# Lending a matmul accumulator bank between two sums in a fused attention and mixture-of-experts kernel

## The chip, the cores and the metric

The kernel runs on one core of one Trainium2 chip. The metric is the device time of one execution in microseconds (us). TensorE (PE) multiplies and writes only into PSUM, which here is used as eight banks of 128 x 512 fp32. VectorE (DVE) and ScalarE (ACT) read results out of PSUM; GpSimd (POOL) works on SBUF; SyncE (SP) issues DMAs. Each engine takes its instructions in the order in which the program lists them. Engines wait for one another by semaphores.

## The reference

Agent attention over 4 batches of 11456 tokens of width 128, with 49 agents per batch, and then a mixture of 8 experts of which each token takes one:

```python
a2k = softmax(scale * agents @ k.T);  agent_v = a2k @ v        # 49 x 128 per batch
q2a = softmax(scale * q @ agents.T);  x = q2a @ agent_v        # 11456 x 128 per batch
logits = x @ w_gate;  e = argmax(logits);  g = softmax(logits)[e]
out = g * (relu(x @ w1[e]) @ w2[e])                            # w1: 128 x 1024, w2: 1024 x 128
```

All inputs and outputs are fp32.

## The kernel before

Each batch is cut into 12 chunks: eleven of 1024 tokens and a last one of 192. For one chosen expert per batch the product of agent values and `w1` is formed once (`Ah` and `Al`, the high and low fp16 halves), so that layer 1 of a token is a product with its 49 attention weights. Those weights stand in `M`. Tokens that chose another expert are done in blocks at the end.

**The main stream.** The function `experts(b)` goes over 23 groups of four 128-token tiles (the last of a batch holds two 96-token tiles), and within a group over 8 slices `f` of the 1024 hidden units. One pair of group and slice is a *step*: 184 steps a batch, 736 in all. A step is `layer1` (two 512-column matmuls into a bank `ph`, L1535 and L1536; then ACT writes the high half of `hh`, L1538, and DVE the low half, L1539, which frees the bank) and, five steps later (`LAG = 5`), `layer2` (12 matmuls of 128 columns into the bank `py`, L1553). Eight steps make one *sum* in `py`. When a sum is complete DVE drains it with one multiplication, `yo<-py,cs` (L1566).

**The side work.** While batch b is in the main stream, the attention of the next batch is worked on between its steps: for each chunk the scores of k and q (`kscores`, `qscores`: 24 matmuls into one bank), the values (`values`, 24 matmuls) and the gate products (`logits`, 8 matmuls). ACT drains a k score, DVE drains the other three. The q scores and gate products of batch 0 fall into batch 0's own stream.

**The banks.** `psH` has four banks for `ph`; `psY` has two, tag `y`, that its pool hands out in turn to the sums; `psS` has the last two, tag `s`, for side work and for small products (`small_ps`). The function `either` gives a side tile its bank. In batch 0 (`both` true) it takes `s` and `y` by turns; in all other batches always `s`. `TFL` flips the turn once at step time 104.2.

**What sets the order.** Every piece of side work is put in a heap at a time counted in steps (`at(t, ...)`, `now[0]`), and the program is traced in that order. The tile framework then puts the traced instructions in a fixed order per engine: one that waits for a bank in the framework's own account of time lets later ones that are ready go ahead. The order stands before the program starts; on the chip an engine waits at an instruction whose bank is still held, and all behind it wait too.

Of the kernel before, what the change touches and what calls it, by code (L numbers as in the profile page):

```python
# [12 lines left out]
F32 = mybir.dt.float32  # L13
# [6 lines left out]
PSUM = bass.MemoryType.PSUM  # L20

P = 128
# [6 lines left out]
LDB, HLB, SPB, MP, HP, NH, NY = 11, 6, 14, 6, 8, 4, 2  # L29
# [25 lines left out]
UDL = 1.5  # L55
LHH, LATER = 11, (1, 4, 6)
ES, SV0 = 2, 1.7
TFL = 104.2
VD3, UD0, QD9 = 1.3, 1.2, 1.5
TM2 = 1.7  # L60
QM0, QG0 = (-145.5, -141.85, -137.3), ("K", "V", "V")
# [34 lines left out]
def agent_moe_kernel(ctx, tc, q, k, v, agents, wg, w1, w2, out):  # L96
# [34 lines left out]
    both = cpool.tile([P, A], F32, name="both")  # L131
# [45 lines left out]
    main = ExitStack()  # L177
# [11 lines left out]
    NKP = -(-NSE // UG) + -(-NSL // UG)  # L189
    keep = pl("keep", 2)  # L190
    psH = main.enter_context(tc.tile_pool(name="psH", bufs=NH, space=PSUM))
    psY = main.enter_context(tc.tile_pool(name="psY", bufs=NY, space=PSUM))
    psS = main.enter_context(tc.tile_pool(name="psS", bufs=8 - NH - NY, space=PSUM))

    def small_ps():
        return psS.tile([P, 512], F32, tag="s", name="ps_small")

    turn = [0]

    def either(both, p0, t0, p1, t1):  # L200

        turn[0] += 1
        p, t = (p1, t1) if both and turn[0] % 2 else (p0, t0)
        return p.tile([P, 512], F32, tag=t, name="ps_" + t)

    def chunk_view(x, c):
        t0, p, t = chunks[c]
# [93 lines left out]
    now, count = [0], [0]  # L301

    def at(t, f, *a):
        count[0] += 1
        heapq.heappush(events, (t, count[0], f, a))
# [10 lines left out]
    def attention(b):  # L316
        st = state[b]
        base = b * steps
        first, last = b == 0, b + 1 == B

        how = {}
# [233 lines left out]
        S = [None] * NCK  # L555
        MX = {}

        def kpiece(i0, i1, behind):
            if i0 == 0:
                S[0] = psY.tile([P, 512], F32, tag="y", name="ps_y")  # L560
            with queued(behind):
                scores("k", 0, S[0], i0, i1)

        def kscores(c):
            _, p, t = chunks[c]
            if b == 1 and c == 0:
                ps = S[0]
                scores("k", c, ps, KP[1])
            else:
                ps = either(first, psS, "s", psY, "y")  # L570
                scores("k", c, ps)
            S[c] = spool.tile([P, 8, A], F32, tag="S", name="S")
            sv = S[c][:p, :t, :]
            pv = ps[:p, :t * A].rearrange("p (t a) -> p t a", a=A)
            m = 1.0 if how["k", c] == "X" else SC["k", c][1][:p, :1]
            if first and c % 4 == 1:
                nc.vector.tensor_scalar(sv, pv, m, None, op0=ALU.mult)
            else:
                nc.scalar.activation(sv, pv, AF.Copy, scale=m)
            if PKM and not first:  # L580
                if c == 0:
                    MX["x"] = one.tile([P, 8, A], F32, tag="mx", name="mx")
                    nc.vector.tensor_scalar(MX["x"], pv, m, None, op0=ALU.mult)
                else:
                    x = MX["x"][:p, :t, :]
                    nc.vector.scalar_tensor_tensor(x, pv, m, x, op0=ALU.mult, op1=ALU.max)
# [48 lines left out]
        AV = {}  # L635
# [32 lines left out]
        def values_wide(c):  # L668

            _, p, t = chunks[c]  # L670
            x, sc = load("v", c), S[c]
            if c == 0:
                AV["acc"] = one.tile([P, D + 1], F32, tag="acc", name="acc")
                AV["pv"] = psY.tile([P, 512], F32, tag="y", name="pv")
            ps, sv = AV["pv"], sc[:p].rearrange("p t a -> p (t a)")
            for i in range(t):
                r, n = 64 * (i % 2), 64 if i + 1 < t else A
                gate["VL"] = nc.tensor.matmul(ps[r:r + n, :D + 1], sv[:, i * A:i * A + n], x[:p, i, :], start=(c == 0 and i < 2),
                                 stop=(c == NCK - 1 and i >= t - 2))
            if c == NCK - 1:  # L680
                with queued("HQ"):
                    nc.vector.tensor_copy(AV["acc"][:AR], ps[:AR, :D + 1])

        def values(c):
            if how["v", c] == "F":
                values_wide(c)
                return
            _, p, t = chunks[c]
            ps = either(first, psS, "s", psY, "y")
            (vh, vl), eh = TT.pop(("v", c)), EH.pop(c)  # L690
            for i in range(t):
                pairs = [(eh[:p, 0, i, :], vh[:p, i, :]), (eh[:p, 1, i, :], vh[:p, i, :]), (eh[:p, 0, i, :], vl[:p, i, :])]
                for n, (e, v_) in enumerate(pairs):
                    nc.tensor.matmul(ps[:, :A], v_, e, start=(i == 0 and n == 0), stop=(i == t - 1 and n == len(pairs) - 1))
            o = ps[:, :A]
            div = SC["v", c][1][:P, :1]
            if c == 0:
                AV["acc"] = one.tile([P, D], F32, tag="acc", name="acc")[:, :A]
            acc = AV["acc"]
            if c == 0:  # L700
                nc.vector.tensor_scalar(acc, o, div, None, op0=ALU.mult)
            else:
                nc.vector.scalar_tensor_tensor(acc, o, div, acc, op0=ALU.mult, op1=ALU.add)
# [95 lines left out]
        def qscores(c):  # L799
            _, p, t = chunks[c]  # L800
            if first and c < NQ:
                ps = psY.tile([P, 512], F32, tag="y", name="ps_y") if c else psH.tile([P, 512], F32, tag="h", name="ps_q")
                if c == 2:
                    scores("q", c, ps, 0, 4)
                    at(QM0[c] - 0.1, qpiece, ps)
                else:
                    scores("q", c, ps)
                at(base + QM0[c], qmax, c, ps)
                return
            ps = either(first and how["q", c] != "X", psS, "s", psY, "y")  # L810
            scores("q", c, ps)
            qmax(c, ps)

# [56 lines left out]
        def logits(c):  # L870
            _, p, t = chunks[c]
            if c == 0:
                route_tiles()
            ps = either(first, psS, "s", psY, "y")
            for i in range(t):
                nc.tensor.matmul(ps[:p, i * E2:(i + 1) * E2], Ms[c][:, i, :p], AV["Gs"], start=True, stop=True)
            pv = ps[:p, :t * E2].rearrange("p (t s e) -> p t e s", s=2, e=E + 1)
            nc.vector.tensor_reduce(RT["L"][:p, c * 8:c * 8 + t, :], pv, axis=AX.X, op=ALU.add)  # L878
# [180 lines left out]
        for c in range(NCK):  # L1059
            t = KS1[c] - base if b == 1 and c < len(KS1) else ks + kt * c  # L1060
            use(t, "k", c)
            prepare(t, "k", c)
            s = KS2[c] - base if b == 1 and c in KS2 else t + kl
# [10 lines left out]
        for c in range(NCK):  # L1074
            t = tv + vt * c
# [5 lines left out]
            at(base + t + dl, kexp2, c)  # L1081
            at(base + t + 2 * dl, kexp3, c)
            at(base + t + vl + (VD3 if b > 1 and c == 3 else 0), values, c)
        if first:
            at(TFL, lambda: turn.__setitem__(0, turn[0] + 1))
        ta = tv + vt * (NCK - 1) + vl + 2
        te = tv + vt * (NCK - 1) + 2 * dl
        if not first:
# [12 lines left out]
        for c in range(NCK):  # L1101
            if first and c < NQ:
                t, ql_ = QS0[c], QL0[c]
            else:
                t = (Q0 + QC * (c - 3) if first and c > 2 else QA + QB * c if c < 3 else
                     QA + 2 * QB + (QB3 if last else QC) * (c - 2))
                ql_ = KLL if last and c > 2 else KL
                if not first and c < 2:
                    t, ql_ = (t - QE, ql_) if c == 0 else (t, ql_ + QL1)
# [304 lines left out]
    def block_layer2(u, hf):  # L1414

        wv = wsp[u, 1].rearrange("p s (t d) -> p s t d", d=D)
        if hf == 0:
            bh[u] = psY.tile([P, 512], F32, tag="y", name="pyb")
        py, hh = bh[u], bh.pop((u, hf))
        for t in range(hf * 4, hf * 4 + 4):  # L1420
            x = hh[:, :, t % 4 * P:(t % 4 + 1) * P]
            nc.tensor.matmul(py[:, :D], x[:, 0, :], wv[:, 0, t, :], start=(t == 0), stop=False)
            nc.tensor.matmul(py[:, :D], x[:, 0, :], wv[:, 1, t, :], start=False, stop=False)
            nc.tensor.matmul(py[:, :D], x[:, 1, :], wv[:, 0, t, :], start=False, stop=(t == FT - 1))
# [99 lines left out]
    def experts(b):  # L1524
        st = state[b]
        hs = {}
        pys = {}
# [16 lines left out]
        def layer2(g, f):  # L1544

            c, h, n = groups[g]
            p = chunks[c][1]
            if f == 0:
                pys[g] = psY.tile([P, 512], F32, tag="y", name="py")
            py, x = pys[g], hs.pop((g, f))  # L1550
            for i in range(n):
                o, s = py[:p, i * D:(i + 1) * D], slice(i * p, (i + 1) * p)
                mm_ = lambda l, r, **k: nc.tensor.matmul(o, l, r, skip_group_check=True, **k)  # L1553
                mm_(x[:, 0, s], st['w2h'][:, f, :], start=(f == 0 and i == 0), stop=False)
                mm_(x[:, 0, s], st['w2l'][:, f, :], start=False, stop=False)
                mm_(x[:, 1, s], st['w2h'][:, f, :], start=False, stop=(f == FT - 1))
            if f == FT - 1:
                todo.append(g)
# [168 lines left out]
```

## Time and profile before

| | us |
|---|---|
| median of three runs | 1076.61 (1076.25 to 1080.18) |
| the profiled execution | 1071.08 |
| span of its instructions | 1069.3 |
| time around the span | 1.78 |

In the profile an engine is busy while it executes; what it waited for before an instruction is its idle time, with the instruction that ended it. Main stream and side work run from about 70 us to 985 us after the start; before that batch 0's keys and values are worked on, after it the blocks of tokens that are left over. TensorE's granted clock is full (1.00) up to 980 us and 0.95 on average in the 89 us after that.

### The profile page before, as it was taken

How to read it: one execution, taken by the hardware profiler on the slowest of the kernel's cores; microseconds unless marked ns; L12 is line 12 of the kernel's file. 1: busy time of each engine (PE TensorE's matmuls, PEld its weight loads, DVE VectorE, ACT ScalarE, POOL GpSimd, SP SyncE). 2: the span in 40 equal slices, each digit the busy share in tenths (PEclk: the TensorE clock that was granted, in tenths of full speed). 3: DMA queues.
4: the chain of work that ended last, by engine and by line, in shares of the span. 5: the costliest groups of instructions: out<-in, count | busy, mean ns of one | idle time of the engine just before them, and what ended most of it. 6: DMA issues, size and time to landing. Idle time of an engine off the chain costs nothing.

```text
span 1069.3 us, 35681 instructions
## 1 busy us (share of the span) xinstructions
PE 1006.5 (94%) x14586; PEld 816.8 (76%) x14586; DVE 977.8 (91%) x2256; ACT 828.2 (77%) x1519; POOL 251.5 (24%) x457
## 2 busy tenths in 40 slices
PE   7989999999999999999999999999999999999986
PEld 7878778777777877777777877777778778767885
DVE  5789999999999998999999998999999999899893
ACT  6668887888788878988788877988677667667674
POOL 1100001236100101334200001333200235171283
PEclk9999999999999999999999999999999999999999
DMA  9889998534699997544699997544556664434550
GB/s 322 273 228 216 203 215 188 140 96 150 166 233 227 222 190 198 159 148 163 160 242 220 225 190 201 154 160 144 144 132 145 159 142 102 148 116 147 170 194 16
DMA packets 265368, 188.39 MB, mean 176 GB/s; under 512 B 207129, under 2 KB 231282, under 8 KB 265200
## 3 DMA queue, kind: packets, MB, share of 16 engines
q1 hardware_dynamic: 263632, 183.82, 67.2%
q0 software_dynamic: 1568, 2.25, 1.1%
q8 instruction: 115, 1.88, 0.7%
q14 instruction: 53, 0.43, 0.1%
HBM read 99.75 MB, written 36.43 MB: 127 GB/s over the span
## 4 chain that ended last, share of the span: by engine, by line
DVE 43%; PE 28%; ACT 12%; issue 9%; DMA 3%; POOL 3%; SPq 0%; POOLq 0%; DVEq 0%; ACTq 0%
DVE hh L1539 16%; PE py L1553 13%; DVE hl L449 8%; PE ph L1535 5%; PE ph L1536 4%; ACT hh L1538 3%; ACT hl L445 3%; DVE yo L1566 3%; ACT jk L407 2%; DVE S L640 1%; DVE mq L824 1%; DVE mx L603 1%; DMA ld<-in_q_dram 1%; DVE E L828 1%; POOL out_dram L1437 1%
## 5 line engine op out<-in xcount | busy, mean ns | idle before, releaser
L1553 PEld LDWEIGHTS <-hh 128*128 128x128 f16 x8640 | 543.5, 98 | 165.5 <-issue 2.0
L1553 PE MATMUL py<-w2h,hh 128*128 128x128 f16 (+1 forms) x5760 | 601.8, 219 | 1.4 <-DVE Ld L878 0.9
L1553 PE MATMUL py<-w2l,hh 128*128 128x128 f16 (+1 forms) x2880 | 520.2, 219 | 0.0
L1539 DVE SCALAR_TENSOR_TENSOR hh<-ph,hh 128x512 f16<-128x512 f32 (+1 forms) x736 | 478.2, 668 | 21.8 <-ACT hh L1538 19.6
L1538 ACT ACTIVATE hh<-ph 128x512 f16<-128x512 f32 (+1 forms) x736 | 410.0, 581 | 96.5 <-PE ph L1536 90.2
L1535 PE MATMUL ph<-M,Ah 128*128 128x512 f16 (+1 forms) x736 | 274.0, 372 | 21.0 <-DVE hh L1539 20.4
L1536 PE MATMUL ph<-M,Al 128*128 128x512 f16 (+1 forms) x736 | 274.1, 373 | 0.0
L449 DVE SCALAR_TENSOR_TENSOR hl<-ld,mul,hl 128x1024 f16<-128x1024 f32 (+1 forms) x113 | 138.9, 1230 | 14.8 <-ACT hl L445 14.2
L445 ACT ACTIVATE hl<-ld,mul 128x1024 f16<-128x1024 f32 (+1 forms) x114 | 124.3, 1091 | 34.9 <-DVE mul L257 34.3
L407 ACT ACTIVATE jk<-ld 128x1024 f16<-128x1024 f32 (+1 forms) x122 | 122.2, 1001 | 6.1 <-DMA ld<-in_k_dram 4.1
L260 POOL TENSOR_SCALAR div<-hb,bits 128x1 int32<-128x1 int32 (+1 forms) x86 | 25.4, 295 | 378.6 <-DVE hb L253 372.7
L1536 PEld LDWEIGHTS <-Al 128*128 128x128 f16 x736 | 71.7, 97 | 28.9 <-issue 27.2
L1535 PEld LDWEIGHTS <-Ah 128*128 128x128 f16 x736 | 73.4, 100 | 2.0 <-issue 1.4
L1566 DVE TENSOR_TENSOR yo<-py,cs 128x512 f32<-128x512 f32 (+1 forms) x92 | 61.6, 670 | 0.9 <-PE py L1553 0.9
L657 POOL TENSOR_TENSOR es<-es,S 128x392 f32<-128x392 f32 (+1 forms) x33 | 32.2, 976 | 110.1 <-ACT S L645 99.1
L550 PE MATMUL ps_s<-agh,hT 128*128 128x49 f16 x572 | 51.8, 184 | 1.8 <-DMA hT<-hl 1.8
L551 PE MATMUL ps_s<-agl,hT 128*128 128x49 f16 x572 | 51.6, 184 | 0.0
L552 PE MATMUL ps_s<-agh,hT 128*128 128x49 f16 x572 | 51.6, 184 | 0.0
L550 PEld LDWEIGHTS <-hT 128*128 128x128 f16 (+1 forms) x590 | 47.9, 97 | 4.3 <-issue 2.1
L551 PEld LDWEIGHTS <-hT 128*128 128x128 f16 (+1 forms) x590 | 46.7, 96 | 0.6
L552 PEld LDWEIGHTS <-hT 128*128 128x128 f16 (+1 forms) x590 | 46.4, 96 | 0.0
L645 ACT ACTIVATE S<-S,ln 128x392 f32<-128x392 f32 (+1 forms) x48 | 27.6, 597 | 21.9 <-DVE S L640 21.7
(328 smaller groups left out, 1385.7 us busy)
## 6 DMA issues: line engine op xcount, KB each, us to landing
ld<-in_k_dram SPq DMA_DIRECT2D x44, 512.0 KB
ld<-in_v_dram SPq DMA_DIRECT2D x44, 512.0 KB
ld<-in_q_dram SPq DMA_DIRECT2D x44, 512.0 KB
out_dram<-yo SPq DMA_DIRECT2D x88, 256.0 KB
w2e<-in_moe_w_dram SPq DMA_DIRECT2D x18, 512.0 KB
w1e<-in_moe_w_dram SPq DMA_DIRECT2D x17, 512.0 KB
exps<-E SPq DMA_DIRECT2D x44, 196.0 KB
wn<-in_moe_w_dram SPq DMA_DIRECT2D x16, 512.0 KB
```

The source lines that it names most:

```text
L407: nc.scalar.activation(jk[:p, :t * D], x[:p, :t, :].rearrange("p t d -> p (t d)"), AF.Square, accum_out=ss[:p])
L445: nc.scalar.activation(hi[:p, :t, :], x[:p, :t, :], AF.Copy, scale=m)
L449: nc.vector.scalar_tensor_tensor(lo[:p, :t, :], x[:p, :t, :], m, hi[:p, :t, :], op0=ALU.mult, op1=ALU.subtract)
L550: nc.tensor.matmul(o, x[:, 0, i, :p], AG["h"], start=True, stop=False)
L551: nc.tensor.matmul(o, x[:, 0, i, :p], AG["l"], start=False, stop=False)
L552: nc.tensor.matmul(o, x[:, 1, i, :p], AG["h"], start=False, stop=True)
L1535: x1 = nc.tensor.matmul(ph[:, :nn], st['Ah'][:, f, :], m, start=True, stop=False)
L1536: nc.tensor.matmul(ph[:, :nn], st['Al'][:, f, :], m, start=False, stop=True)
L1538: x2 = nc.scalar.activation(hh[:, 0, :nn], ph[:, :nn], AF.Relu)
L1539: x3 = nc.vector.scalar_tensor_tensor(hh[:, 1, :nn], ph[:, :nn], 0.0, hh[:, 0, :nn], op0=ALU.max, op1=ALU.subtract)
L1553: mm_ = lambda l, r, **k: nc.tensor.matmul(o, l, r, skip_group_check=True, **k)
L1566: nc.vector.tensor_tensor(yo[:p, :n, :], py[:p, :n * D].rearrange("p (i d) -> p i d", d=D), cs.unsqueeze(2).broadcast_to([p, n, D]), op=AL ...
```

## The change

The pool `psY` becomes two tags of one buffer each, `y0` and `y1`, and the program itself alternates between them (`bank_y`). Each sum notes the step time at which it starts (`since`). From the first sum on, `either` looks at the clock of steps: between 1 and 3.3 steps after the start of a sum, and at least 3 steps after the last loan, a side tile gets the bank of the sum before (`1 - ybank`); otherwise it gets a bank of `psS`. That holds in all batches. Before the first sum the turns are as they were. The flip at `TFL` is gone.

```diff
-TFL = 104.2
+YW = 1, 3.3, 3
...
-    psY = main.enter_context(tc.tile_pool(name="psY", bufs=NY, space=PSUM))
+    psY = main.enter_context(tc.tile_pool(name="psY", bufs=1, space=PSUM))
...
-    turn = [0]
-
-    def either(both, p0, t0, p1, t1):
+    turn, ybank, lent, since = [0], [0], [-9], [None]
+
+    def bank_y(name, flip=True):
+        if flip:
+            ybank[0] = (ybank[0] + 1) % NY
+        return psY.tile([P, 512], F32, tag=f"y{ybank[0] if flip else 1 - ybank[0]}", name=name)
+
+    def either(both):
 
         turn[0] += 1
-        p, t = (p1, t1) if both and turn[0] % 2 else (p0, t0)
-        return p.tile([P, 512], F32, tag=t, name="ps_" + t)
+        if since[0] is None:
+            return bank_y("ps_y") if both and turn[0] % 2 else psS.tile([P, 512], F32, tag="s", name="ps_s")
+        if YW[0] <= now[0] - since[0] <= YW[1] and now[0] - lent[0] >= YW[2]:
+            lent[0] = now[0]
+            return bank_y("ps_y", False)
+        return psS.tile([P, 512], F32, tag="s", name="ps_s")
...
-            ps = either(first, psS, "s", psY, "y")
+            ps = either(first)
...
-        if first:
-            at(TFL, lambda: turn.__setitem__(0, turn[0] + 1))
...
             if f == 0:
-                pys[g] = psY.tile([P, 512], F32, tag="y", name="py")
+                pys[g] = bank_y("py")
+                since[0] = now[0]
```

From the first sum on 163 side tiles go through `either`. Before, 9 of them that come behind the first sum's start sit in `psY`, all in batch 0; now 47 are lent a bank, in all four batches. The matmuls, the drains, the DMAs and their sizes are the same. On the order of the engines little moves: SP's is unchanged, and 20 of the 163 side tiles stand elsewhere between the steps, 18 of them later (by up to two steps) and 2 earlier.

Numbers in the rows below are those of the buffers; line numbers differ since lines were added. First TensorE in sum 41 (batch 1), at the values of chunk 10 of batch 2, tile 10971. `py` is the running sum, `hl` the values, `eh` the weights. Before:

```order
L1553 MATMUL py_10930<-w2l_6553,hh_10807 128x128
L1553 LDWEIGHTS hh_10807
L1553 MATMUL py_10930<-w2h_6552,hh_10807 128x128
L694 LDWEIGHTS hl_10697
L694 MATMUL ps_s_10971<-eh_10751,hl_10697 128x49
```

And now:

```order
L1561 MATMUL py_10930<-w2l_6553,hh_10807 128x128
L1561 LDWEIGHTS hh_10807
L1561 MATMUL py_10930<-w2h_6552,hh_10807 128x128
L703 LDWEIGHTS hl_10697
L703 MATMUL ps_y_10971<-eh_10751,hl_10697 128x49
```

Nothing moved; the tile's bank is now that of sum 40. Second VectorE at the drain of that sum, `py_10711`. Before:

```order
L449 SCALAR_TENSOR_TENSOR hl_10895<-ld_10449,mul_10873,hl_10895 96x256
L1539 SCALAR_TENSOR_TENSOR hh_10907<-ph_10904,hh_10907 128x512
L1566 TENSOR_TENSOR yo_10928<-py_10711,cs_6625 128x512
L1539 SCALAR_TENSOR_TENSOR hh_10925<-ph_10922,hh_10925 128x512
L1539 SCALAR_TENSOR_TENSOR hh_10946<-ph_10943,hh_10946 128x512
```

And now:

```order
L458 SCALAR_TENSOR_TENSOR hl_10895<-ld_10449,mul_10873,hl_10895 96x256
L1546 SCALAR_TENSOR_TENSOR hh_10907<-ph_10904,hh_10907 128x512
L1574 TENSOR_TENSOR yo_10928<-py_10711,cs_6625 128x512
L1546 SCALAR_TENSOR_TENSOR hh_10925<-ph_10922,hh_10925 128x512
L1546 SCALAR_TENSOR_TENSOR hh_10946<-ph_10943,hh_10946 128x512
```

The drain keeps its place. Third TensorE in sum 17 (batch 0), at the values of chunk 8 of batch 1, tile 5288. Before it stands at the end of a step, behind a small product:

```order
L1553 MATMUL py_5249<-w2h_1187,hh_5106 128x128
L422 LDWEIGHTS ones16_67
L422 MATMUL ps_small_5280<-ss_5239,ones16_67 128x1
L694 LDWEIGHTS hl_5005
L694 MATMUL ps_s_5288<-eh_5052,hl_5005 128x49
```

And now:

```order
L1561 MATMUL py_5249<-w2h_1187,hh_5161 128x128
L1561 LDWEIGHTS hh_5161
L1561 MATMUL py_5249<-w2l_1188,hh_5161 128x128
L1561 LDWEIGHTS hh_5161
L1561 MATMUL py_5249<-w2h_1187,hh_5161 128x128
L703 LDWEIGHTS hl_5005
L703 MATMUL ps_y_5288<-eh_5052,hl_5005 128x49
```

It moved into the next step, behind three of that step's twelve matmuls.

## Rows read from the trace of the kernel before

**Rows 1.** The page: busy time of the engines, and the chain that ended last.
```profile
PE 1006.5 (94%) x14586; PEld 816.8 (76%) x14586; DVE 977.8 (91%) x2256; ACT 828.2 (77%) x1519; POOL 251.5 (24%) x457
...
DVE 43%; PE 28%; ACT 12%; issue 9%; DMA 3%; POOL 3%; SPq 0%; POOLq 0%; DVEq 0%; ACTq 0%
```

**Rows 2.** Busy time by stretch: four batches' main stream, then their sum.
```profile
core 0: us, PE busy (x) PEld busy (x) DVE busy (x) ACT busy (x) POOL busy (x), PEclk, DMA share, GB/s
70.00:307.00 237.00, 225.98 (x3360) 180.53 (x3360) 225.25 (x515) 196.62 (x356) 47.85 (x90) 1.00 0.75 181
...
sum 915.00, PE 875.93 PEld 698.35 DVE 867.08 ACT 730.35 POOL 203.29; mean PE 218.98 PEld 174.59 DVE 216.77 ACT 182.59 POOL 50.82
```

**Rows 3.** Whom TensorE waited for from 70 to 985 us: total, times, longest.
```profile
PE ph L1535 <- DVE hh L1539: 20.4, 40, 1.3
PE ps_s L694 <- DVE Ld L878: 3.0, 5, 0.8
...
PE ps_s L694 <- DVE E L828: 1.4, 2, 0.7
```

**Rows 4.** Timeline of TensorE: waits for a bank. In brackets: idle before, releaser.
```profile
125.43 0.22 PE L1553 MATMUL py<-w2h,hh 128*128 128x128 f16 x1 [0.93 <-DVE Ld L878]
...
212.43 0.23 PE L694 MATMUL ps_s<-eh,hl 128*128 128x49 f16 x3 [0.26 <-DVE Ld L878]
...
222.46 0.20 PE L550 MATMUL ps_y<-agh,hT 128*96 128x49 f16 x1 [0.70 <-DVE yo L1566]
...
277.77 0.31 PE L720 MATMUL ps_small<-e,ones 128*128 128x49 f32 x1 [0.76 <-DVE acc L703]
...
457.83 0.25 PE L694 MATMUL ps_s<-eh,hl 128*128 128x49 f16 x3 [0.67 <-DVE E L828]
...
464.70 0.21 PE L694 MATMUL ps_s<-eh,hl 128*128 128x49 f16 x2 [0.80 <-DVE Ld L878]
```

**Rows 5.** Timeline: start of a side tile on TensorE, and the preceding sum's drain.
```profile
506.33 0.77 PE L694 MATMUL ps_s<-eh,hl 128*128 128x49 f16 x24
...
508.40 0.67 DVE L1566 TENSOR_TENSOR yo<-py,cs 128x512 f32<-128x512 f32 x1
...
846.40 0.35 PE L876 MATMUL ps_s<-Gs,M 128*128 128x18 f16 x8
...
846.95 0.70 DVE L1566 TENSOR_TENSOR yo<-py,cs 128x512 f32<-128x512 f32 x1
...
339.26 0.19 PE L550 MATMUL ps_s<-agh,hT 128*128 128x49 f16 x1
...
339.59 0.68 DVE L1566 TENSOR_TENSOR yo<-py,cs 128x512 f32<-128x512 f32 x1
```

**Rows 6.** The same where the tile moves: TensorE's new neighbour, and the drain.
```profile
254.26 0.22 PE L1553 MATMUL py<-w2h,hh 128*128 128x128 f16 x1
...
255.66 0.68 DVE L1566 TENSOR_TENSOR yo<-py,cs 128x512 f32<-128x512 f32 x1
...
107.68 0.38 PE L1536 MATMUL ph<-M,Al 128*128 128x512 f16 x1
...
108.80 0.69 DVE L1566 TENSOR_TENSOR yo<-py,cs 128x512 f32<-128x512 f32 x1
...
329.20 0.69 DVE L1566 TENSOR_TENSOR yo<-py,cs 128x512 f32<-128x512 f32 x1
...
329.84 0.22 PE L1553 MATMUL py<-w2h,hh 128*128 128x128 f16 x1
```

**Rows 7.** Timeline of TensorE: waits for a `ph` bank behind those places.
```profile
260.40 0.38 PE L1535 MATMUL ph<-M,Ah 128*128 128x512 f16 x1 [0.89 <-DVE hh L1539]
...
344.96 0.38 PE L1535 MATMUL ph<-M,Ah 128*128 128x512 f16 x1 [0.52 <-DVE hh L1539]
...
508.53 0.38 PE L1535 MATMUL ph<-M,Ah 128*128 128x512 f16 x1 [0.33 <-DVE hh L1539]
...
514.12 0.38 PE L1535 MATMUL ph<-M,Ah 128*128 128x512 f16 x1 [0.53 <-DVE hh L1539]
```

More of the change, by code (lines that the diff above doesn't have):

```diff
@@ L559, in kpiece @@
             if i0 == 0:
-                S[0] = psY.tile([P, 512], F32, tag="y", name="ps_y")
+                S[0] = bank_y("ps_y")
             with queued(behind):
@@ L673, in values_wide @@
                 AV["acc"] = one.tile([P, D + 1], F32, tag="acc", name="acc")
-                AV["pv"] = psY.tile([P, 512], F32, tag="y", name="pv")
+                AV["pv"] = bank_y("pv")
             ps, sv = AV["pv"], sc[:p].rearrange("p t a -> p (t a)")
@@ L688, in values @@
             _, p, t = chunks[c]
-            ps = either(first, psS, "s", psY, "y")
+            ps = either(first)
             (vh, vl), eh = TT.pop(("v", c)), EH.pop(c)
@@ L801, in qscores @@
             if first and c < NQ:
-                ps = psY.tile([P, 512], F32, tag="y", name="ps_y") if c else psH.tile([P, 512], F32, tag="h", name="ps_q")
+                ps = bank_y("ps_y") if c else psH.tile([P, 512], F32, tag="h", name="ps_q")
                 if c == 2:
@@ L809, in qscores @@
                 return
-            ps = either(first and how["q", c] != "X", psS, "s", psY, "y")
+            ps = either(first and how["q", c] != "X")
             scores("q", c, ps)
@@ L873, in logits @@
                 route_tiles()
-            ps = either(first, psS, "s", psY, "y")
+            ps = either(first)
             for i in range(t):
@@ L1417, in block_layer2 @@
         if hf == 0:
-            bh[u] = psY.tile([P, 512], F32, tag="y", name="pyb")
+            bh[u] = bank_y("pyb")
         py, hh = bh[u], bh.pop((u, hf))
```

## The prediction

> **What bounds the kernel now.** I read the page first, for which engine could set the pace. The reader is to see two engines that are almost full, TensorE at 94% and VectorE at 91%, and a chain of work that goes through both, 43% VectorE and 28% TensorE [rows 1]. An average over the whole span hides the stages, so the busy time by stretch comes next: over the main stream, 70 to 985 us, TensorE is busy for 875.93 of 915 us and VectorE for 867.08 [rows 2]. TensorE therefore idles 39 us there and VectorE 48, and nothing that only moves idle time about can bring more than that. The clock is full in all of it, so no part of the 39 us is a slow clock.
>
> The third view says whom TensorE waited for. The largest entry is VectorE's low half of `hh`, 20.4 us in 40 waits: all four `ph` banks are full and VectorE is behind [rows 3]. The waits that this change is about are far smaller: a side tile, a small product or a sum that finds its bank not yet drained. So the two engines take turns at being the late one, and a wait that is taken from one place can come back at the next `ph`.
>
> **What the change takes away.** In the timeline I looked for every wait of TensorE on a PSUM bank other than `ph`, and asked of each whether the bank's two tenants still share it. Eight go. A sum that waited for gate products standing in its bank, 0.93 us; values behind gate products, 0.26; a q score that stood in a sum's bank, 0.70; a small product behind the last values of a batch, 0.76; and, in batch 1, values behind q scores, 0.67, and values behind gate products, 0.80 [rows 4]. The last two come again in batch 2 at 0.68 and 0.80; they are part of the totals of 1.4 and 3.0 us in the list of waits [rows 3]. Together 5.60 us. The other bank waits stay, since their tiles keep a common bank.
>
> **What it adds.** Now 47 side tiles stand in the bank of the sum before, and none of them can start until VectorE has drained that sum. This is a wait that nearly no side tile had before, and what is queued behind it on TensorE is everything: the next `layer1`, hence ACT's and VectorE's halves of `hh`, and the running sum. VectorE's drain keeps its place in its order at nearly all sums, so the trace of before tells when the bank will be free; and 29 of the 47 tiles did not move by any part of a step, so it tells when TensorE will ask for it.
>
> The clearest place is sum 41. The values of chunk 10 started at 506.33 us, and the drain of sum 40 ran from 508.40 to 509.07 [rows 5]: the same tile will wait 2.74 us. A batch later the same pair stands 2.75 us apart. In the last batch the gate products at 846.40 meet a drain that ends at 847.65, 1.25 us [rows 5]. Ten more unmoved tiles come early by 0.12 to 1.01 us, 5.07 us in all; the row shown is one of the largest, scores at 339.26 against a drain that ends at 340.27 [rows 5]. Two that moved are clear too. At sum 17 the tile now follows three matmuls of a step that starts at 254.15, the last of them at 254.26, and the drain ends at 256.34: about 2.0 us. At sum 3 the gate products come behind the `layer1` matmul of 107.68, which ends at about 108.06, and the drain ends at 109.49: 1.45 us [rows 6]. These fifteen places make 2.74 + 2.75 + 1.25 + 5.07 + 2.0 + 1.45 = 15.3 us.
>
> Eight more moved and may or may not wait. An example is the scores at sum 24: the drain starts at 329.20 and ends at 329.89, and TensorE's next matmul of that step began at 329.84 [rows 6], so the wait is 0.05 us if TensorE is as late as that and more if it is early. Three of the eight lie at the short last sum of a batch, where the steps have half as many matmuls and the loan, counted in steps, is over sooner in time: there the lent tile's own drain may make the next sum late. Bounds for the eight together, by the same subtraction at either end of the gap that the tile was put into: 0.8 and 7 us. I take 3, nearer the low end, because the framework set these tiles behind the drain by its own account and 24 loans below show that it is often right. The sum of what is added is 18.3 us. The remaining 24 loans cost nothing: their drain was over, or they waited before as they will now.
>
> **What comes back.** A TensorE that was held for a drain gives VectorE time, and then waits less for the next `ph`. Behind the place at 254 us TensorE waited 0.89 us for `ph` at 260.40, behind 339 us 0.52, behind 506 us 0.33 and 0.53 [rows 7]; such waits within 20 us behind the added ones make 6.7 us when none is counted twice or for more than the wait ahead of it. That is the lower bound. The upper bound, 14, is what the whole 20.4 us could give if VectorE never ran dry in between. It does run dry at times (48 us of idle), so I take the middle, 10.5. What is removed is subject to the same: a TensorE that arrives earlier meets a VectorE that is no earlier. I let 1.4 of the 5.6 us return, with bounds 0 and 2.6.
>
> Neither the drain's length nor any count of instructions changes, SP's queue is as it was, and the flip at `TFL` was a number and no instruction: these cost nothing and need no cover.
>
> **The sum.** 18.3 - 10.5 - 5.6 + 1.4 = +3.6 us on the profiled execution of 1071.08 us: 1074.7. The median of the runs stands at 1076.61, a factor 1.0052 above that execution, which gives 1080.2; I predict 1080. With all terms at their good ends: 16.1 - 14 - 5.6 = -3.5, or 1073. With all at their bad ends: 22.3 - 6.7 - 5.6 + 2.6 = +12.6, or 1089. A difference below 0.5% (5.4 us) can hardly be told from no change here.
>
> **Rivals.** *The loans are nearly free and the kernel is faster.* All waits that I add hang on when VectorE reaches a drain. If holding TensorE once lets VectorE catch up for good, each later drain comes earlier. From about 1.3 us earlier only four places are left of the thirteen unmoved and two moved ones, with some 3.7 us, and `ph` waits give that back; the 5.6 us are gained, less 1.4 at most: -4 to -6, about 1071. For it speaks the 20.4 us that TensorE loses to VectorE's lateness [rows 3]; against it that VectorE has no more than 48 us of idle in 915 [rows 2], so that it hardly catches up for long. [...]
>
> *The waits add up and the kernel is slower.* The mechanism is the one above with less coming back: TensorE waits for a drain, and before it comes to a `ph` that would have made it wait anyhow, VectorE has run out of `hh` to work on and is late as well. Then the end moves by the wait. The place to look at is sum 41 and its twin. With the bad ends the time is 1089; it decides against no change from +5.4 us on, that is, when less than 8.7 us come back. For it: TensorE does most of its idling between such places and not right behind them; only 0.86 of the 2.74 us find a `ph` wait nearby [rows 7].
>
> *The change does not do what it says.* Lent banks could go to tiles that never lacked one, and gains and losses both vanish. For it: 143 of 163 side tiles keep their place between the steps. The time would be 1076 to 1077.
>
> **Chances.** My forecast (a few us up, within 0.5%) 0.31; no effect 0.15; faster 0.22; slower by over 0.5% 0.32. That makes 0.22 faster, 0.46 same, 0.32 slower. For 8 in 10 the range has to take in the faster rival and most of the slower: 1070 to 1087. The likeliest case by itself spans 1077 to 1082.
>
> **What would show it.** In the profile after, TensorE's waits of `ps_y` for `yo` should make 10 to 20 us (before: 1.4 in two waits), with 2 to 3 us at sums 41 and 64 and about 2 at sum 17; its waits of values for gate products or q scores should be gone at the six places shown; its waits for `ph` should be 7 to 12 us less than 20.4. VectorE's busy time should not change. I am wrong on the size if the waits for `yo` stay below 5 us (then the drains are earlier than before, and the faster rival holds), or if they are as predicted and the waits for `ph` do not fall (then the slower one does). I am wrong altogether if the difference lies outside the main stream, since no tile before the first sum or after the last one has moved.

## The result and the profile after

The changed kernel is a little slower. Measured in turns on one chip, nine runs of each, it took 1085.25 us in the median (1080.9 to 1090.25) against 1077.33 (1076.25 to 1081.2): a ratio of 1.0066 with a 95% interval of 1.0049 to 1.0082, or about +7.1 us. The forecast was 1080; the time lies in its range and on the side of the rival in which the waits add up. The profiled execution took 1084.07 us.

The page after, its busy times and its chain, answers to [rows 1]:

```profile
PE 1010.1 (93%) x14586; PEld 817.0 (75%) x14586; DVE 981.2 (91%) x2256; ACT 830.5 (77%) x1519; POOL 250.5 (23%) x457
...
DVE 40%; PE 31%; ACT 12%; issue 8%; DMA 4%; POOL 3%; another core or an unknown queue 0%; SPq 0%; POOLq 0%; ACTq 0%; DVEq 0%
```

The work is the same and both engines are as full as before; the chain now goes more through TensorE. The page does not tell where 7 us went. The list of what TensorE waited for from 70 us to 1000 us (total, times, longest) tells more, and answers to [rows 3]:

```profile
PE ph L1542 <- DVE hh L1546: 12.7, 25, 1.1
PE ps_y L703 <- DVE yo L1574: 10.5, 7, 2.6
PE ps_y L885 <- DVE yo L1574: 3.4, 4, 1.7
PE ps_y L559 <- DVE yo L1574: 3.1, 6, 0.8
...
PE ps_s L703 <- DVE Ld L887: 1.1, 2, 0.6
```

There are 17 waits of a lent tile for the drain of the sum that stands in its bank (`yo`), 17.0 us together, where there were two of 1.4 us; the waits for `ph` have shrunk. The three longest are where the prediction put them, at the values tiles of sums 17, 41 and 64. In TensorE's timeline (start, duration; in brackets the idle time before it and what ended it) the tile of sum 41 reads

```profile
505.75 0.38 PE L1542 MATMUL ph<-M,Ah 128*128 128x512 f16 x1 [0.19 <-DVE hb L262]
...
509.65 0.77 PE L703 MATMUL ps_y<-eh,hl 128*128 128x49 f16 x24 [2.63 <-DVE yo L1574]
...
518.05 0.35 PE L381 MATMUL ps_small<-sa,ones 128*128 128x1 f32 x2 [0.63 <-DVE rs L732]
```

Against the 2.74 us that [rows 5] gave, it waited 2.63. The waits for `ph` at 508.53 and 514.12 [rows 7] have no counterpart: the held TensorE finds `ph` free for the rest of the sum.

**Where the 7 us are.** A span ends after many stages, so I cut it at starts of sums (the first `layer2` matmul of a sum). The first 78 sums hold all the long waits. The windows view gives for them length, TensorE's busy time, and, after ACT and POOL, the granted clock; first the two profiles of the kernel before, then the one after, then a second one of after:

```profile
71.77:883.22 811.45, 776.18 (x11582) 619.91 (x11581) 770.28 (x1781) 656.15 (x1186) 161.63 (x300) 1.00 0.74 179
71.73:884.89 813.16, 777.08 (x11581) 620.09 (x11581) 770.71 (x1778) 657.49 (x1186) 162.11 (x300) 1.00 0.75 178
```

```profile
70.86:889.42 818.56, 779.62 (x11581) 620.95 (x11581) 772.63 (x1778) 658.18 (x1186) 161.61 (x300) 1.00 0.73 176
```

```profile
71.79:892.59 820.80, 782.27 (x11582) 623.50 (x11582) 771.32 (x1778) 658.57 (x1186) 162.33 (x300) 0.99 0.74 176
```

With the idle time before each of TensorE's instructions in that stretch added up by what ended it (us):

| the first 78 sums | length | busy | idle | `ph` | `yo` | other VectorE | rest |
|---|---|---|---|---|---|---|---|
| before, first profile | 811.45 | 776.18 | 35.27 | 18.4 | 1.4 | 11.5 | 4.0 |
| before, second | 813.16 | 777.08 | 36.08 | 16.9 | 1.4 | 11.6 | 6.2 |
| after, first | 818.56 | 779.62 | 38.94 | 11.4 | 16.9 | 8.1 | 2.6 |
| after, second | 820.80 | 782.27 | 38.53 | 9.6 | 16.6 | 7.8 | 4.5 |

In the mean of two profiles each the stretch is 7.4 us longer, as much as the timing shows (+7.1). Only 3.1 us of that are idle time of TensorE. The other 4.3 are TensorE being busy longer with the same instructions.

**The clock.** Most of these 4.3 us go with a slower clock. In the stretch behind the wait at sum 64, the windows view of after shows a mean granted clock of 0.62 over 4.5 us, between stretches at 1.00:

```profile
749.00:753.00 4.00, 1.26 (x14) 0.90 (x14) 3.86 (x9) 3.55 (x8) 3.60 (x10) 1.00 0.00 0
753.00:757.50 4.50, 4.48 (x53) 3.37 (x53) 3.76 (x8) 3.45 (x6) 3.64 (x13) 0.62 0.18 62
757.50:761.00 3.50, 3.50 (x52) 2.79 (x49) 3.09 (x5) 1.79 (x3) 1.54 (x3) 1.00 0.32 62
```

and the timeline shows what TensorE did there:

```profile
510.26 0.38 PE L1542 MATMUL ph<-M,Ah 128*128 128x512 f16 x1
...
753.02 0.77 PE L703 MATMUL ps_y<-eh,hl 128*128 128x49 f16 x24 [2.63 <-DVE yo L1574]
753.63 0.58 PE L1542 MATMUL ph<-M,Ah 128*128 128x512 f16 x1
754.01 0.63 PE L1543 MATMUL ph<-M,Al 128*128 128x512 f16 x1
```

TensorE had idled 2.63 us; some 0.6 us after the tile began the granted clock falls to half (0.50 over 753.7 to 757.1, in the windows view), and a `layer1` matmul takes 0.63 us instead of 0.38 (the first row is one at full clock). The mean of 0.62 over 4.5 us, too, makes some 3.4 us at half. The second profile of after has three such stretches: beside the waits at sums 17 and 64, and beside a wait of 2.24 us for the DMA of `hT` at 554 us. The second profile's window of sum 17 is

```profile
257.00:261.50 4.50, 3.83 (x48) 3.28 (x48) 4.29 (x10) 2.92 (x6) 4.26 (x6) 0.62 0.68 184
```

Sum 17 is thus the same wait, 2.36 us, with and without the slow stretch. The sum itself took 13.85 us without it and 15.43 with it, 1.58 apart; by the start of sum 20, two sums on, 0.97 of that is left (34.95 and 35.92 us from the start of sum 17; before 35.16, where sum 17 by itself took 12.35).

### The profile page after: what moved, and what is told of

Read it like the earlier page. It is cut to its first block, busy times and chain, and to the rows that moved or that the text cites. A ratio compares the mean times of both kernels' runs of the same rounds, so it can differ in the third digit from the quotient of the medians.

```text
span 1082.4 us, 35678 instructions
## 1 busy us (share of the span) xinstructions
PE 1010.1 (93%) x14586; PEld 817.0 (75%) x14586; DVE 981.2 (91%) x2256; ACT 830.5 (77%) x1519; POOL 250.5 (23%) x457
## 4 chain that ended last, share of the span: by engine, by line
DVE 40%; PE 31%; ACT 12%; issue 8%; DMA 4%; POOL 3%; another core or an unknown queue 0%; SPq 0%; POOLq 0%; ACTq 0%; DVEq 0%
DVE hh L1546 16%; PE py L1561 14%; DVE hl L458 7%; PE ph L1542 5%; PE ph L1543 5%; ACT hh L1545 3%; ACT hl L454 3%; ACT jk L416 3%; DVE yo L1574 3%; POOL out_dram L1444 1%; DVE mq L833 1%; DMA ld<-in_q_dram 1%; DVE S L649 1%; DVE mx L612 1%; DMA hT<-hl 1%
## 5 line engine op out<-in xcount | busy, mean ns | idle before, releaser
L654 ACT ACTIVATE S<-S,ln 128x392 f32<-128x392 f32 (+1 forms) x48 | 27.6, 596 | 21.6 <-DVE S L649 21.6
L850 ACT ACTIVATE E<-E,ln,div 128x392 f32<-128x392 f32 (+1 forms) x45 | 31.0, 688 | 16.1 <-DVE E L837 15.2
L559 PE MATMUL ps_s<-agh,hT 128*128 128x49 f16 x410 | 37.5, 184 | 1.5 <-DMA hT<-hl 0.9
L561 PE MATMUL ps_s<-agh,hT 128*128 128x49 f16 x410 | 37.3, 184 | 0.5 <-issue 0.5
```

Of the source, the lines that this page charges most:

```text
L559: nc.tensor.matmul(o, x[:, 0, i, :p], AG["h"], start=True, stop=False)
L561: nc.tensor.matmul(o, x[:, 1, i, :p], AG["h"], start=False, stop=True)
```

## The experiments

My theory (A): what the change costs is TensorE held at lent tiles for the previous sum's drain. Rival (B): the cost lies in what else changed, the turns of batch 0, the flip at `TFL` that is gone, the moved tiles. The ratios below are to the kernel before on the same chip. *Waits* are TensorE's waits for `yo` at a tile, in the main stream, total and number of those above 0.1 us, from one profile. *Clock* is the mean granted clock of the timed executions, and behind it that of before on the same chip; it is on record for each timed execution.

| kernel | what is lent | ratio [95%] | us | waits | clock (before) |
|---|---|---|---|---|---|
| after | 47 tiles | 1.0066 [1.0049, 1.0082] | +7.1 | 17.1 in 17 | 0.9916 (not on record) |
| e1_values_in_s | no values | 1.0036 [1.0019, 1.0053] | +3.9 | 6.3 in 10 | 0.9943 (0.9944) |
| e2_window_late | later in the sum | 1.0001 [0.998, 1.0023] | +0.1 | 0 | 0.9926 (0.9944) |
| e3_no_loans | nothing | 0.9994 [0.998, 1.0009] | -0.6 | 0 | 0.9940 (0.9944) |
| e4_only_values | 12 values tiles | 1.0013 [0.9998, 1.0029] | +1.4 | 10.5 in 7 | 0.9915 (0.9944) |
| e5_window_wide | 72 tiles | 1.0102 [1.0077, 1.0127] | +11.0 | 21.6 in 25 | 0.9903 (0.9944) |
| e6_store_first | as after, drain traced first | 1.006 [1.0037, 1.0082] | +6.5 | 16.5 in 19 | 0.9907 (0.9944) |
| e7_three_in_s | all but the three longest waits | 1.0028 [1.0012, 1.0044] | +3.0 | 9.5 in 14 | 0.9947 (0.9939) |
| e8_three_only | those three alone | 1.0034 [1.0017, 1.005] | +3.6 | 7.6 in 3 | 0.9909 (0.9939) |
| e9_only_k | k scores | 1.0017 [0.9997, 1.0038] | +1.8 | 1.1 in 2 | 0.9938 (0.9939) |
| e10_free_loans | after less 14 that waited | 0.9984 [0.996, 1.0009] | -1.7 | 3.7 in 5 | 0.9952 (0.9939) |

**Is it the loans, and their time in the sum?** Two kernels change one line:

```diff
-YW = 1, 3.3, 3
+YW = 4, 5.5, 3      # e2_window_late
+YW = 9, 9, 3        # e3_no_loans
```

and one takes the values out of the loans (in `values`; gate products and scores stay):

```diff
-            ps = either(first)
+            ps = psS.tile([P, 512], F32, tag="s", name="ps_s")
```

> Values always take a psS bank; q and k scores and gate products are still lent the bank of the sum before. Theory A (the loss is TensorE held at lent tiles for the drain of the sum before): the 10.5 us of waits of values for yo go, some 6 us of such waits stay with the other tiles, and 2 to 3 us of waits of values behind gate products return; 1079 to 1082 us. Rival B (the loss comes from the turns in batch 0 that are gone and from the changed order): no change, 1084 to 1086. Rival C (the long wait at sum 64 makes the clock fall for 3.4 us, and the rest are gaps that come by chance): the clock stays full after 70 us, 1083 to 1084.

> The window of a loan is 4 to 5.5 steps after the start of a sum (not 1 to 3.3), so that the drain is over when TensorE comes to the lent tile. Theory A: waits of ps_y for yo under 2 us (17 in the changed kernel); time at or below that of before, 1073 to 1079. Rival B: the banks are still given otherwise than before, 1083 to 1087. A danger: lent tiles drained so late that the next sum waits for them; then waits of py for a drain of more than 3 us.

> The window is never open: after the first sum every side tile takes a psS bank, in batch 0 too, where before they took turns. Theory A: no wait for yo in ps_y at all, a few us of waits at psS banks as before; 1076 to 1080. Rival B (the turns of batch 0 were worth the time): 1083 to 1087, with the loss before 310 us.

The kernel before was also profiled once more beside them:

> The kernel before, unchanged, for a second profile of it. If the gaps of about 1 us that end with no releaser on TensorE between 890 and 940 us, and a fall of the clock inside the main stream, belong to the change, this profile has none of them; if they come by chance, it may have some. 1075 to 1081 us.

Without loans the time is that of before, within 0.1% in the middle of the interval: the turns, the flip and the banks of their own cost nothing that can be told. The moved tiles are not tested by this, since all but two of them stand in their old places again when nothing is lent; in e10_free_loans, below, at least 15 of the 20 still stand where the change put them, and it is no slower than before. With both, B falls. With loans that come late in a sum, when the drain is over, there is no wait for `yo` and no cost. Without the values the waits are 6.3 us and the cost is about half.

The late loans also take bank waits away, though not the same ones as the change. The list of TensorE's waits of e2_window_late:

```profile
PE ph L1542 <- DVE hh L1546: 20.7, 37, 1.7
...
PE ps_s L703 <- DVE Ld L887: 1.6, 2, 0.8
...
PE ps_s L703 <- DVE E L837: 1.4, 2, 0.7
```

Of the 3.0 us for `Ld` [rows 3] 1.6 are left, and the 1.4 for `E` as well: these are four of the eight waits that the change took away, so this kernel has only part of that gain. `ph` is as long as before, and the time does not move. The second profile of before took 1079.56 us, with 19.0 us at `ph` in the same list: the entry that nearly all of the argument rests on repeats within 1.4 us.

**More and fewer of the same waits.** More:

```diff
-YW = 1, 3.3, 3
+YW = 0.5, 4, 0      # e5_window_wide
```

fewer, of one kind (scores and gate products go to `psS` once the sums have begun):

```diff
-                ps = either(first)
+                ps = psS.tile([P, 512], F32, tag="s", name="ps_s") if since[0] is not None else either(first)
```

and the same waits with the drain traced ahead of the next step's `layer1`:

```diff
-            if i < len(seq):
-                layer1(*seq[i])
             if todo:
                 store(todo.pop(0))
+            if i < len(seq):
+                layer1(*seq[i])
```

> The complement of the first run: after the first sum only values are lent a bank (12 tiles); scores and gate products take psS. Theory A: waits of values for yo of 9 to 11 us, no other waits for yo, and a share of the loss like the one that the first run took away, +2.5 to +4 us: 1081 to 1083. If the loss were not additive over the tiles that wait (rival: VectorE is given time and pays it all back), no change from before, 1078 to 1080.

> The window is 0.5 to 4 steps and two loans need no distance, so 72 tiles in place of 47 are lent, many before the drain. The drains of the trace before put about 30 us of waits for yo against their places (about 18 for the changed kernel). Theory A, at 0.4 to 0.5 us of time for each us of such wait: +12 to +15 us, 1090 to 1094. Rival (what is lost beyond a few us comes back at the ph banks): under 1087.

> The loans as changed, but each finished sum is drained ahead of that step's layer 1 in the program's text, so that yo stands up to one hh (0.6 us) earlier on VectorE. Theory A: each of the 17 waits for yo is up to 0.6 us shorter, 9 to 13 us in all in place of 17, and 1080 to 1083; unless the framework also puts the lent tiles earlier, then 17 us and no change, 1084 to 1087.

> The changed kernel, for a second profile. The waits for yo should be the same to a tenth (17.1 us in 17). If the fall of the clock for 3.4 us at sum 64 is caused by the wait of 2.6 us ahead of it, it is there again, or at sum 41, which has the same wait; if it came by chance, not.

The wide window is the slowest kernel (+11.0 us, where 12 to 15 were expected from 30 us of waits that became 21.6), and its list shows a second kind of wait, of a lent tile for ACT's drain of a k score in the same bank:

```profile
PE ph L1542 <- DVE hh L1546: 13.0, 25, 1.4
PE ps_y L703 <- DVE yo L1574: 11.5, 9, 2.6
PE ps_y L559 <- DVE yo L1574: 7.8, 12, 1.3
PE ps_y L559 <- ACT S L588: 2.8, 5, 0.8
```

Tracing the drain earlier was a miss: the waits for `yo` are 16.5 us instead of 17.1 and the time is that of after. At sums 41 and 64 neither the tile nor the drain moved (waits of 2.62 and 2.63 us); at sum 17 and some other places the lent tile stands three to seven matmuls earlier too. The kernel with values alone is cheaper than its 10.5 us of waits would be by proportion (10.5 / 17.1 x 7.1 = 4.4; its interval ends at +3.1). So the length of the waits is not the whole of it, as far as an interval from -0.2 to +3.1 us can tell. The second run of after took 1088.32 us and repeats the waits (17 of them, 16.9 us); what it adds is the clock, above.

**The three long waits, the others, and the loans that do not wait.** With `LONG = (1, 8), (2, 10), (3, 10)`, the batch and chunk of the three values tiles, one kernel takes these three out and one keeps only them:

```diff
-            ps = either(first)
+            ps = psS.tile([P, 512], F32, tag="s", name="ps_s") if (b, c) in LONG else either(first)   # e7_three_in_s
+            ps = bank_y("ps_y", False) if (b, c) in LONG else either(first)                           # e8_three_only, with YW = 9, 9, 3
```

The third lends a bank to k scores alone, with `values`, `qscores` and `logits` sent to `psS` as in the diffs above. The fourth leaves out the loans at the 14 step times whose tiles had waited in after (13 for `yo`, one 0.97 us for VectorE's `hb`):

```diff
             lent[0] = now[0]
-            return bank_y("ps_y", False)
+            if round(now[0], 1) not in HELD:
+                return bank_y("ps_y", False)
```

> The changed kernel, but the three tiles with the longest waits (values of chunk 8 in sum 17, of chunk 10 in sums 41 and 64; 2.4 to 2.6 us each) take a psS bank. Theory A: waits for yo of 9 to 10 us in place of 17. Theory D (a wait of TensorE of 2.4 us or more lets the clock fall to half for 3.4 us, which costs 1.6 us more): no fall of the clock near sums 17, 41 and 64 any more; A and D together 1080 to 1082. If neither the waits nor the clock at these places matter for the end: 1085 to 1087.

> The complement: no loans but for these three tiles. Theory D: waits for yo of 7 to 8 us in three, the clock falls behind at least two of the three, +2 to +5 us: 1080.5 to 1083.5. Without D and with all of it paid back at ph: 1078 to 1080, and no fall of the clock there.

> Only k scores are lent a bank. In the changed kernel they wait for yo in two places, 0.9 us in all, while scores and gate products together cost 3.9 us in the first run. Theory A: waits for yo under 3 us and no loss that can be told, 1077 to 1080. Rival (a lent bank costs without a wait, since tiles moved by a step delay what needs them): +1.5 us or more, 1080 to 1083.

> The loans of the changed kernel without 14 of those that waited for yo; four that wait no longer than the tile did for its psS bank before stay lent. Waits for yo of 3 to 5 us in about four, and the bank waits that the change took away still gone. Theory A: at or a little under the kernel before, 1075 to 1079. Rival (loans cost by the order alone): 1081 to 1084.

Three tiles of 163 cost about half of it, and the rest costs the other half: 3.6 + 3.0 = 6.6 against 7.1, each known to some 1.8 us either way. The list of e8_three_only shows that the waits at side tiles are as before, `Ld` included, while `ph` has given back about 4 of the 7.6 us (15.5, against 20.4 and 19.0 in the two profiles of before):

```profile
PE ph L1543 <- DVE hh L1547: 15.5, 30, 1.3
PE ps_y L704 <- DVE yo L1575: 7.6, 3, 2.6
...
PE ps_s L704 <- DVE Ld L888: 3.0, 5, 0.8
```

Without the waiting loans (e10_free_loans) nothing can be told from before. That kernel still lends some thirty tiles a bank and has `Ld` at 1.1 us:

```profile
PE ph L1544 <- DVE hh L1548: 17.8, 37, 1.3
...
PE ps_s L705 <- DVE Ld L889: 1.1, 2, 0.6
```

So loans without waits neither cost nor bring anything that 0.25% either way can show. With k scores alone the question stays open: +1.8 us, with an interval from -0.3 to +4.1, fits both the theory (no loss that can be told) and its rival (+1.5 or more). No version here beats the kernel before.

**The clock in the timed executions.** Theory D expected the clock to fall behind at least two of the three long waits in e8_three_only, and nowhere near them in e7_three_in_s. In the profiles it missed: one of the three waits has a fall beside it in the first, and in the second it falls at sum 41 without the wait. A profile is one execution, though, and the column *clock* of the table averages 6 to 12 (those of before 17 to 35; the standard error of each mean is 0.0008 or less). It covers the whole execution, stretches outside the main stream included. The five kernels that hold the three long waits stand at 0.9903 to 0.9916; before stands at 0.9939 and 0.9944, and the kernels without these waits at 0.9938 to 0.9952, but for e2_window_late at 0.9926. One stretch of 3.4 us at half clock takes, by estimate, 0.0016 off the mean of such an execution (1.7 of 1076 us), so e8_three_only has about two stretches more than before, and after nearly as many if the kernel before had on its chip what it had on the other three. The long waits thus do bring the clock down, on average and not each time. By the same column e1_values_in_s and e7_three_in_s lose their 3.9 and 3.0 us with no loss of clock: there the shorter waits, or what hangs on them, are what is paid. It is no price list: e4_only_values loses as much clock as e8_three_only and only 1.4 us, and e2_window_late loses some clock and no time.

**What a wait comes to, place by place.** Between the start of the sum that waits and that of a later sum where the difference has settled, the kernels took longer than the first profile of before by (us; *half* is a stretch at half clock in that place, *hl* a VectorE instruction that took over 0.7 us longer, which the next part shows):

| place | after | after, second | e4_only_values | e8_three_only |
|---|---|---|---|---|
| sums 3 and 4, wait 1.69 | +0.33 | +0.33 | -1.11, no loan | -1.10, no loan |
| sums 17 to 19, wait 2.36 | -0.21 | +0.76 half | +0.76 half | +0.76 half |
| sums 41 and 42, wait 2.63 | +1.19 hl | +1.19 hl | +3.29 half, twice as long | +1.18 hl |
| sums 64 to 67, wait 2.63 | +2.05 half, hl | +1.69 half | +1.65 half | +1.31 hl |

A wait of 2.36 us at sum 17 costs nothing by the start of sum 20 where nothing else happens. Where it is not given back there is something beside it. The kernel without the three loans, e7_three_in_s, shows the price of the clock by itself: at sums 41 and 42 it has no wait for `yo` and yet +1.65 us, with a stretch at half clock there. Two smaller places make up most of the remainder: sum 0, +0.82 in both profiles of after and in e9_only_k, and -0.01 in the kernels that lend no bank to a k score (e3_no_loans, e4_only_values, e8_three_only); and sums 74 to 77 at the end, +1.72 and +1.54 with a lent tile that waits 0.71 us for `yo`, where the second profile of before has +0.39. (In sum 73 a lent tile waits 0.97 us for `hb`, and the sum is as long as before, since a wait of 1.32 us for `ph` is gone.) Between sums 45 and 53, with the stretch at half clock beside the wait for `hT`, the second profile of after is 2.3 us longer than before.

**Sum 41 in windows.** The first 6.30 us, which hold the wait, and from there to the next sum; VectorE's busy time is the third. After:

```profile
504.73:511.03 6.30, 3.47 (x60) 2.75 (x59) 6.16 (x15) 5.31 (x12) 5.43 (x18) 1.00 0.10 35
511.03:518.70 7.67, 7.04 (x92) 5.48 (x89) 7.48 (x15) 5.49 (x11) 4.18 (x10) 1.00 0.33 66
```

Before:

```profile
504.19:510.49 6.30, 5.76 (x87) 4.51 (x86) 6.16 (x15) 5.34 (x12) 5.43 (x18) 1.00 0.10 36
510.49:516.97 6.48, 5.00 (x63) 3.80 (x61) 6.40 (x15) 5.19 (x11) 4.27 (x10) 1.00 0.40 81
```

In the first 6.30 us VectorE does the same 15 instructions in the same 6.16 us, whether TensorE stands still or not: VectorE sets the pace here, and this is how a wait of TensorE comes back. In the second part it has again 15 instructions, but 7.48 us of work instead of 6.40. Its timeline shows which one grew. After, VectorE and then POOL:

```profile
512.87 2.47 DVE L458 SCALAR_TENSOR_TENSOR hl<-ld,mul,hl 128x1024 f16<-128x1024 f32 x1
...
512.78 1.47 POOL L1166 TENSOR_TENSOR C<-C,cp 128x704 f32<-128x704 f32 x1
```

Before:

```profile
512.18 1.28 DVE L449 SCALAR_TENSOR_TENSOR hl<-ld,mul,hl 128x1024 f16<-128x1024 f32 x1
...
512.26 2.54 POOL L1159 TENSOR_TENSOR C<-C,cp 128x704 f32<-128x704 f32 x1
```

Before, VectorE began 0.08 us ahead, took 1.28 us, and POOL's instruction took 2.54. After, POOL began 0.09 us ahead, took 1.47, and VectorE's took 2.47. The one that comes second ends 1.1 to 1.3 us after the first has ended, as if it had begun there (before 514.80 - 513.46 = 1.34; after 515.34 - 514.25 = 1.09). All 14 profiles have this pair at sums 41 and 64. Where VectorE starts first (16 cases) POOL's instruction ends 1.33 or 1.34 us after VectorE's; where POOL starts first (12 cases, those of the six profiles with the three long waits) VectorE's ends 1.08 us after POOL's. In the rows above the later one took 1.1 to 1.2 us longer than the same one where it came first (VectorE's 2.47 against 1.28, POOL's 2.54 against 1.47). What holds it up no run here shows. The price at sum 41 has a bound: TensorE's last wait there, 0.63 us for `rs` at 518.05, stands behind the slow `hl`, so up to 0.63 of the 1.19 us go to it and the rest to the wait itself. No kernel took POOL's instruction away from there, so this part is read from rows and not tested.

## Why the prediction was right, and where not

**The added waits.** 18.3 us were forecast, 15.4 more than before were measured (16.8 against 1.4 in the mean of the table above). Sum 41: 2.74 against 2.63; sum 64: 2.75 against 2.63; sum 17: 2.0 against 2.36; sum 3: 1.45 against 1.69. Reading when a bank comes free and when TensorE asks for it from the trace of before worked, tile by tile, and e3_no_loans, e8_three_only and e10_free_loans show that these waits carry the loss.

**What comes back.** 10.5 us were forecast, with a lower bound of 6.7; the waits for `ph` fell by 7.2 (17.7 to 10.5). This term was mis-sized, by taking the middle of the bounds. Its local form was wrong in the other direction: "only 0.86 of the 2.74 us find a `ph` wait nearby" made me count on little return at sum 41. There 1.44 came back (2.63 less 1.19): the two `ph` waits of [rows 7] (0.86), 0.31 of a small product's wait for VectorE (0.94 before, 0.63 now), and the rest in TensorE's busy time (10.77 to 10.52 in the windows).

**What is removed.** 5.6 less 1.4 were forecast; the other waits in the table fell by 5.1, of which 1.5 are in the column *rest*, where single DMA waits come and go from profile to profile (for `hT`, in the lists from 70 to 1000 us, 1.8 us in one and 2.9 in four before, 0.9 in one and 2.6 in two after). But "a TensorE that arrives earlier meets a VectorE that is no earlier" holds for much of it. Before, two values tiles of batch 1 waited 0.67 us behind q scores and 0.80 [rows 4]; now those q scores and the second tile wait for the drain instead, in TensorE's timeline of after

```profile
454.65 0.18 PE L559 MATMUL ps_y<-agh,hT 128*128 128x49 f16 x1 [0.76 <-DVE yo L1574]
...
466.47 0.20 PE L703 MATMUL ps_y<-eh,hl 128*128 128x49 f16 x1 [0.89 <-DVE yo L1574]
```

and a batch later the same pair waits 0.75 and 0.90 us. e10_free_loans, which keeps the gain together with these four short waits, is not faster than before. No kernel here keeps the whole gain without any wait for `yo`.

**The sum.** 15.4 - 7.2 - 5.1 = +3.1 us, the idle time found above, where +3.6 was forecast. That it is so near is luck in part: less was added, less came back, more was removed.

**The step that failed** is the one on what costs nothing: "Neither the drain's length nor any count of instructions changes", and with it that the clock, full before, would stay so. It left out the term that makes up the other half of the result: TensorE is busy 4.3 us longer with the same instructions. One stretch at half clock in the first profile of after and three in the second, two in the mean at 1.6 us, make 3.2 of them; about 1 us of busy time I cannot place (e1_values_in_s and e10_free_loans, with no such stretch, show as much: 778.1 and 777.9 us, against 776.6 in the mean of before). The mean clock of the timed executions, 0.9916 against 0.9939 to 0.9944 for the kernel before on the other chips, says that between one and two such stretches more are usual.

**The rivals.** The faster one fell: VectorE did not come to its drains earlier by anything like the 1.3 us of that rival, and the waits are as long as the trace of before said. That loans go to tiles that never lacked a bank is true of those that do not wait (e10_free_loans), not of the change. The slower one was the outcome, with its condition met (less than 8.7 us came back), but nearly half of its price is the clock, which it did not name. "VectorE's busy time should not change": over the 78 sums it is 770.3 and 770.7 us before, 772.6 and 771.3 after; the 1.2 us of `hl` are in it.

## What to carry to other kernels

Before a buffer is lent between two uses, read from the trace when its last reader ends and when the borrower comes: TensorE took its work in the program's order, so a borrower's wait (2.63 us at sum 41) held everything behind it, and three tiles of 163 made about half of the loss here. Freeing a bank for an engine that waits for a late partner brought nothing here (e10_free_loans, a ratio of 0.9984 [0.996, 1.0009]); the lateness turned up at the next place where the two meet. A wait that seems to be given back may still be paid for, because the clock falls beside it (here beside 11 of 18 such waits) or because it changes which of two engines' instructions comes first (here VectorE's then took 2.47 us instead of 1.28); so look at clock and instruction lengths behind a new wait, and not only at waits.

## What the runs showed of the hardware

**The clock beside single waits.** In the six profiles (of five kernels) with these three loans, 18 waits of 2.36 to 2.64 us stand at the long places in a stream that is otherwise full; beside 11 of them the granted clock fell to half for some 3.4 us (once twice as long), and beside 7 it did not, at the same tile and in the same kernel. Of the waits for the DMA of `hT`, those of 2.19 and 2.46 us passed without it, and those of 1.87, 2.24, 2.45 and 2.82 us had it, as had one of 1.97 us for the DMA of `M` (e7_three_in_s at 381 us). None of the waits between 1.5 and 1.8 us, for VectorE or a DMA, had it. Twice it fell with no wait of that size in front (e7_three_in_s at 518 us, e2_window_late at 74 us). What decides between the 11 and the 7 no run here shows.

**Gaps that nothing ends.** Between 885 and 945 us TensorE loses about 2 us three times, in steps with idle time put down to "issue", in most profiles, the second of before included:

```profile
890.77 0.38 PE L1535 MATMUL ph<-M,Ah 128*128 128x512 f16 x1 [0.52 <-issue]
...
892.25 0.22 PE L1553 MATMUL py<-w2h,hh 128*128 128x128 f16 x1 [0.53 <-issue]
```

From sum 78 to the end of the main stream TensorE took 128.5 us in the first profile of before, 134.7 in the second, and 135.2 and 133.3 in those of after. So that first profile, on which the prediction stood, is short by some 6 us there for a reason that the change has no part in, and the comparison above was made over the first 78 sums. The gaps go with the chip: all eight profiles that were taken on two of the chips have them (133.3 to 134.7 us), the four on the third have none (128.5 us in three of them and 130.0 in e7_three_in_s), and on that chip the median of before is 1072.1 us, against 1079.1 and 1078.3. The prediction's factor of 1.0052, 5.5 us, is about their size. What these gaps are the profile does not say.
